# Reordering late products, half-sums and a small norm in a fused linear-attention and GEGLU kernel

## The chip, the cores and the metric

The kernel runs on one core of a Trainium2 chip. The metric is the device time of one launch in microseconds. A core has TensorE (PE in the profile: matrix products into PSUM), VectorE (DVE), ScalarE (ACT, with the gelu and exp functions), GpSimd (POOL, which does not touch PSUM in this kernel) and SyncE (SP, which here only issues DMA transfers). Each engine takes its instructions in the order in which the program writes them for it; between engines they wait for each other.

## The reference

Two stages follow each other. The inputs q, k, v are 8 batches x 8 heads x 576 positions x 64 channels:

```
q_s = softmax(q) over the 64 channels of a head
k_s = softmax(k) over the 576 positions
x   = q_s @ (k_s^T @ v)           # per batch and head, heads side by side: 4608 x 512
out = (gelu(x @ w_gate) * (x @ w_val)) @ w_out      # 512 -> 1536 -> 512
```

All is given and returned in fp32; the kernel multiplies in fp16 and sums in fp32.

## The kernel before, in words

The 4608 rows are done in nine blocks of 512 rows. Blocks 0 to 7 are the first 512 positions (in the kernel's own order) of batches 0 to 7; block 8 collects the 64 remaining positions of all eight batches. The order is 0, 1, ..., 6, 8, 7 (L531). Within a block the hidden layer has 12 columns of 128 (ht[0] to ht[11]), each gelu(g) * v of 512 rows. While a block is in the products with w_gate and w_val, and then in the one with w_out, the attention part of the next batches is interleaved: loads, exp, norms, transposes, the product of keys and values (`unit_kv4`) and x itself (`unit_x4`).

From block 2 on, some hidden columns are made in pairs (k and k+3) by a Strassen-Winograd scheme: seven half-size products instead of eight, at the price of sums beforehand and afterwards. A pair has four steps, written "k.1" to "k.4" (`pair_step`, L630):

- k.1: product 1 into a bank pga, which ScalarE copies to a second bank pgb; product 5 into pgc, of which a snapshot is taken.
- k.2: product 6 into pga, snapshot on ScalarE; product 3 into pgc; VectorE adds (cc, first half).
- k.3: product 7 into pga, VectorE adds (cc, second half, "eq" or "cc" in the profile); product 2 into pgb, from which ScalarE (gelu, glq) and VectorE make the first 256 rows of ht[k] (`final`); then `upper`: ScalarE's gelu on cc, and a 128x512 product by GpSimd (by VectorE for pair 8) that makes rows 256 to 511 of ht[k] and ht[k+3].
- k.4: product 4 into pga, then `final` for the first 256 rows of ht[k+3].

Other columns are made whole ("8g", "8v": `half`, L620): four matmuls each for g and v, gelu on ScalarE, one product on VectorE.

The order of the steps is written out by hand in three strings (L611 to L616): THREE for block 2 (three pairs), FOUR for blocks 3 to 6 (four pairs), SIX for blocks 7 and 8 (six pairs, all columns). `go_on` (L691) walks through a string. Letters in it are places where a list of other work (`plan`, filled by `at`) is run by `ride`; a list may be empty. Four of them matter here: s0, u0, s1, u1 are the half-sums of ht that the product with w_out needs, since that one is a Strassen-Winograd product too (`sum_h`, L566): sj is sum 1 on VectorE and sum 3 on GpSimd, uj is sum 2 on VectorE and sum 4 on GpSimd; j = 1 covers columns 1, 4, 7, 10. The letter t is the DMA transpose of the next batch's normalised q (`unit_td`), and r, in block 6 alone, is the norm of the remaining positions of batch 0 (`norm_rem0`, L268: a VectorE reduce and reciprocal, a GpSimd product) with its DMA transpose (`unit_trem`, L374).

Some work is put off by one step: `live["late"]` holds a function that `go_on` calls after the next item of the string. Two kinds are put off: the `upper` of pair 8 (L680), and the `final` of a k.4 step if the very next item of the string ends in ".1" (L686).

The output stage is `out_strassen` (L728): product 1 into bank a (with the last step or steps k.4 between its matmuls: 2.4 in blocks 3 to 6, 8.4 in blocks 7 and 8), product 2 into b, 5 into c, 6 into a, 3 into c, 7 into a, 4 into a, each of 12 matmuls of 256 columns. `snap` takes a copy of a bank before the next product adds to it; `add` writes rows of the output; the half-sums of columns 2, 5, 8, 11 come between (`last_js`). Product 1 needs ht[0] to ht[5], product 2 needs ht[6] to ht[11], in the order 0, 3, 1, 4, 2, 5. Places NS 0, 1, 2, 4 are where other work rides along: NS 1 is after product 5, NS 2 after product 6. At NS 2 VectorE also makes some of the weight sums (`sum_wgv`) that pairs 7 and 8 of blocks 8 and 7 use.

PSUM has eight banks, handed out in rotation (`big`); a pair's banks are given back by `let_go` when the last reader is written in the program.

Of the kernel before, what the change touches and what calls it, by code (L numbers as in the profile page):

```python
# [18 lines left out]
def kernel(  # L19
# [12 lines left out]
    B, H, S, D = q.shape  # L32
# [16 lines left out]
    NO = NFI // 2  # L49
# [30 lines left out]
    def big(shape, dt, name, hold=False, seed=False):  # L80
        tag = ring.pop(next(i for i, x in enumerate(ring) if x in full) if seed else 0)
        t = ps_big.tile(shape, dt, name=name, tag=tag)
        words = 1
        for n in shape[1:]:
            words *= n
        (full.add if words == 512 and shape[0] == 128 and dt == f32 else full.discard)(tag)
        if hold:
            held[id(t)] = (t, tag)
        else:
            ring.append(tag)  # L90
        return t
# [29 lines left out]
    for i, nm in enumerate("gv"):  # L121
        n = 3 * NO * P
# [472 lines left out]
    def product_gv(i, ps, xt, k, first):  # L595
# [3 lines left out]
        for t, w, nm in ((0, wv_sb, "v"), (1, wg_sb, "g")):  # L599
            ss = ws[(nm, k // NO)]  # L600
            for c in range(2):
# [6 lines left out]

    THREE = ("a 6g l 6v 0.1 9g 0.2 9v w 0.3 7g 0.4 n m 1.1 t 7v 1.2 10g 1.3 s0 10v 1.4 2.1 u0 8g 2.2 s1"  # L611
             " 8v 2.3 u1 11g 2.4 11v x")
    FOUR = ("a 7g l 7v n 0.1 6.1 0.2 6.2 0.3 6.3 m 10g 0.4 6.4 1.1 t 10v 1.2 s0 8g u0 1.3 8v 1.4 r 2.1"
            " 11g s1 2.2 11v 2.3")
    SIX = ("0.1 6.1 0.2 6.2 0.3 6.3 0.4 1.1 6.4 7.1 s0 1.2 7.2 1.3 u0 7.3 1.4 2.1 7.4 8.1 2.2"
           " 8.2 2.3 s1 8.3 u1 2.4")  # L616
    steps = {b: (SIX if b >= B - 1 else THREE if b == 2 else FOUR).split() for b in range(2, B + 1)}
    live = {}

    def half(b, xt, c, nm):  # L620
        t = big([P, 512], f32, "ps" + nm)
        mm_gv(t, wg_sb if nm == "g" else wv_sb, xt, c, range(HP))
        if nm == "g":
            live[c] = ffn.tile([P, 512], f32, name="gl", tag="gl")
            nc.scalar.activation(out=live[c], in_=t, func=ACTF.Gelu)
        else:
            nc.vector.scalar_tensor_tensor(out=ht[:, c, :], in0=t, scalar=_H_SCALE,
                                           in1=live[c], op0=ALU.mult, op1=ALU.mult)
# [62 lines left out]
    def go_on(b, xt, upto=None):  # L691
        while steps[b] and upto != 0:
            x = steps[b].pop(0)
            late = live.pop("late", None)
            if "." in x:
                k, i = x.split(".")
                pair_step(b, xt, int(k), int(i))
                upto = upto - 1 if upto else None
            elif x[-1] in "gv" and x[:-1].isdigit():
                half(b, xt, int(x[:-1]), x[-1])  # L700
            else:
                ride(b, PR, x)
            if late:
                late()
# [3 lines left out]
    def product(i, ps, first, ts=(0, 1), js=range(NO)):  # L708
        for j in js:
            for t in ts:  # L710
                c0, c1 = slice(t * P, (t + 1) * P), slice(256 + t * P, 256 + (t + 1) * P)
                a = {1: ht[:, j, c0], 2: ht[:, NO + j, c0], 3: s4[:, j, c0], 4: ht[:, NO + j, c1],
                     5: sh[1][:, j, c0], 6: sh[2][:, j, c0], 7: ht[:, j, c1]}[i]
                w = {1: wo_sb[:, j, 0:256], 2: wo_sb[:, NO + j, 0:256],
                     3: wo_sb[:, NO + j, 256:512]}.get(i)
                if w is None:
                    w = tw[{4: 4, 5: 1, 6: 2, 7: 3}[i]][:, j]
                nc.tensor.matmul(ps[t], a, w, start=(first and j == js[0] and (  # L718
                    t == ts[0] or ps[t].tensor is not ps[ts[0]].tensor)),
                                 stop=(j == js[-1]), skip_group_check=True)  # L720

    def get_x(b):
        return get_xt(b) if b < B else xtr
# [4 lines left out]
    def out_strassen(b, last):  # L728
        yo = [yop.tile([P, 2, C], f32, name="yo", tag="yo") for _ in range(2)]
        c = (slice(0, 256), slice(256, 512))  # L730
        ps, tiles_ = {}, {}

        def get(nm):
            if last:
                tiles_[nm] = [big([P, 256], f32, "ps" + nm, True) for _ in range(2)]
                ps[nm] = [x for x in tiles_[nm]]
            else:
                tiles_[nm] = [big([P, 2, 256], f32, "ps" + nm, True)]
                ps[nm] = [tiles_[nm][0][:, t] for t in range(2)]

        def parts(nm):
            return [(0, ps[nm][0]), (1, ps[nm][1])] if last else [(slice(0, 2), tiles_[nm][0])]

        def snap(nm, act=False):
            sn = ffn.tile([P, 2, 256], f32, name="sn", tag="gl")
            for n, (t, src) in enumerate(parts(nm)):
                if n or act:
                    nc.scalar.activation(out=sn[:, t], in_=src, func=ACTF.Copy, scale=1.0 / _H_SCALE)
                else:
                    nc.vector.tensor_scalar(out=sn[:, t], in0=src, scalar1=1.0 / _H_SCALE,  # L750
                                            scalar2=None, op0=ALU.mult)
            return sn

        def add(nm, sn, half, col):
            for t, src in parts(nm):
                nc.vector.scalar_tensor_tensor(  # L756
                    out=yo[half][:, t, c[col]], in0=src, scalar=1.0 / _H_SCALE,
                    in1=sn[:, t], op0=ALU.mult, op1=ALU.add)

        js = (0, 1, 2, 3, 4, 5) if b < 2 else (0, 3, 1, 4, 2, 5)  # L760
        get("a")
        four = 2 < b < B - 1
        cut = 3 if four else 4
        product(1, ps["a"], True, js=js[:cut])
        if four:
            pair_step(b, get_x(b), NO // 2 - 1, 4)
            product(1, ps["a"], False, js=js[cut:4])
        ride(b, NS, 0)
        if four:
            ride(b, PR, "u1")  # L770
        if b >= B - 1:
            pair_step(b, get_x(b), NFI - NO // 2 - 1, 4)
        get("b")
        product(1, ps["a"], False, js=js[4:])
        if b > 1 and not last:
            s1 = snap("a", True)
        ride(b, PR, "e")
        sum_h(*last_js(b), (1, 2))
        if b < 2 or last:
            s1 = snap("a")  # L780
        product(2, ps["b"], True, js=js)
        add("b", s1, 0, 0)
        for x in tiles_["b"]:
            let_go(x)
        sum_h(*last_js(b), (4,), "pool" if b > 1 else "dve")
        get("c")
        product(5, ps["c"], True, js=js)
        sum_h(*last_js(b), (3,), "pool" if b > 1 else "dve")
        s5 = snap("c", b == B)
        ride(b, NS, 1)  # L790
        product(6, ps["a"], False, js=js)
        s2 = snap("a", b == B)
        ride(b, NS, 2)
        cut = NO - 1 if 1 < b < B - 2 else NO
        product(3, ps["c"], False, js=js[:cut])
        if cut < NO:
            product(7, ps["a"], False, js=js)
            add("a", s5, 1, 1)
            product(3, ps["c"], False, js=js[cut:])
        add("c", s2, 0, 1)  # L800
        for x in tiles_["c"]:
            let_go(x)
        store_rows(b, 0, yo[0])
        if last:
            finish_last(b, ps["a"], yo[1], s5)
            return
        if cut == NO:
            product(7, ps["a"], False, js=js)
            add("a", s5, 1, 1)
        ride(b, NS, 4)  # L810
        if b == B:
            go_on(B - 1, get_x(B - 1), 1)
        product(4, ps["a"], False, js=js)
        nc.scalar.activation(out=yo[1][:, :, c[0]], in_=tiles_["a"][0], func=ACTF.Copy,
                             scale=1.0 / _H_SCALE)
        let_go(tiles_["a"][0])
        store_rows(b, 1, yo[1])
# [97 lines left out]
    FI, NS, PR = range(3)  # L915
    plan = {}

    def at(b, kind, i, *fns):
        plan.setdefault((b, kind, i), []).extend(fns)

    L = lambda f, *a: (lambda: f(*a))
# [39 lines left out]
    for b in range(2, B):  # L961
        n = b + 1
# [8 lines left out]
            at(b, PR, "e", L(exp, "q", n + 1), L(exp, "k", n + 1))  # L971
    at(4, PR, "l", load_rem0)
    at(4, PR, "e", exp_rem0)
    at(6, PR, "r", norm_rem0, L(unit_trem, 0))
    for b in range(2, B - 1):
        n = b + 1
        at(b, NS, 4, L(unit_x4, n, ("act", "dve"), 0 if n == B - 1 else None))
# [9 lines left out]
    for i, xs_ in (("w", ("g1", "v1", "g2", "v2")), ("x", ("g4", "v4", "g3", "v3"))):  # L987
        for x in xs_:
            at(2, PR, i, L(sum_wgv, x[0], int(x[1]), NO, 1, "pool"))
    for b, x in ((3, "g1"), (3, "g2"), (4, "v1"), (4, "v2"), (5, "g4"), (5, "v4"), (6, "g3"), (6, "v3")):  # L990
        at(b, NS, 2, L(sum_wgv, x[0], int(x[1]), NO + 1, 2))


    def ride(b, kind, i):
        for fn in plan.get((b, kind, i), []):
            fn()

    for b in order:
# [9 lines left out]
        if b > 1:  # L1008
            go_on(b, xt)
# [50 lines left out]
```

## Time and profile before

| | us |
|---|---|
| median of 13 runs | 300.62 |
| lowest, highest | 299.01, 302.50 |
| profiled execution, its own time | 300.53 |
| its span, first to last instruction | 298.7 |
| TensorE busy in the span | 285.1 |
| VectorE busy | 225.9 |
| GpSimd busy | 206.6 |
| ScalarE busy | 194.0 |
| the two weight sums g4, v4 at NS 2 of block 5 (starts) | 198.75, 199.48 |
| norm of batch 0's remainder in block 6 (start of the reduce) | 218.14 |

In the 13 runs the times were 300.53, 299.04, 302.5, 299.17, 299.15, 299.36, 300.77, 300.87, 299.01, 300.7, 302.3, 300.62 and 300.76.

How to read it: the profile's page gives busy times per engine, the clock granted to TensorE in 40 slices, and groups of instructions with the idle time ahead of them and what ended it. Rows in order of time have the start and the length in us, the engine, the source line, the operation, the names it writes and reads, the shapes, and in brackets the idle time before it and what released it. A row may merge several instructions in succession ("x2"). Matmul ends are modelled, so the starts tell more than the lengths. Windows give, for each stretch, its length, the busy time and number of instructions of PE, PEld (weight loads), DVE, ACT and POOL, then the granted clock and the DMA share and rate. Block 2's own steps lie at about 82 to 102 us, its output to 112; blocks 3 to 6 follow every 30 us; block 8 ends its steps at about 252, block 7 at about 284.

### The profile page before, as it was taken

The page shows a single profiled execution, that of the slowest core. Times are in us where ns is not written, and L with a number is a line of the kernel's source. Part 1 is how long each engine was busy: PE and PEld are TensorE (multiplying, and loading weights), DVE is VectorE, ACT ScalarE, POOL GpSimd, SP SyncE. Part 2 cuts the span into 40 slices and gives each one's busy share as a digit, 9 for nine tenths or more (in the row PEclk, how much of TensorE's full clock was granted, in tenths as well). Part 3 has the DMA queues.
Part 4 walks back from the last instruction along what each step waited for, and adds up shares of the span by engine and source line. Part 5 has one row for each costly group of instructions (what it writes and reads, how often), then busy time and mean ns, then how long its engine had stood idle before and what let it go on. Part 6 is the DMA issues. An engine that isn't in the chain of part 4 may idle for free.

```text
span 298.7 us, 6345 instructions
## 1 busy us (share of the span) xinstructions
PE 285.1 (95%) x2449; PEld 204.1 (68%) x2449; DVE 225.9 (76%) x411; ACT 194.0 (65%) x319; POOL 206.6 (69%) x191
## 2 busy tenths in 40 slices
PE   3999999999999999999999999999999998899974
PEld 1544445446766687678767876787678887688864
DVE  2954888978867759768976897689788799449982
ACT  3763467777776398759875987598760777146720
POOL 1558658860599799868986898689875666824570
PEclk9999999999999999999999999999999999799999
DMA  7999999996179307950796069503040300041003
GB/s 223 372 383 390 401 389 395 336 313 195 59 232 346 74 1 248 376 84 0 229 383 112 0 218 383 107 2 143 3 96 2 140 2 1 2 102 41 1 2 140
DMA packets 54622, 51.72 MB, mean 173 GB/s; under 512 B 18496, under 2 KB 50496, under 8 KB 54592
## 3 DMA queue, kind: packets, MB, share of 16 engines
q1 hardware_dynamic: 52864, 49.49, 52.3%
q10 hardware_dynamic: 1728, 1.84, 1.9%
q8 instruction: 19, 0.31, 0.4%
q14 instruction: 11, 0.09, 0.1%
HBM read 37.75 MB, written 9.44 MB: 158 GB/s over the span
## 4 chain that ended last, share of the span: by engine, by line
PE 86%; DVE 7%; ACT 3%; POOL 1%; issue 1%; ACTq 1%; DVEq 0%
PE pga L606 15%; PE psa L718 13%; PE psv L467 12%; PE psg L467 12%; PE pgc L606 8%; PE psc L718 7%; PE psb L718 4%; PE pgb L606 4%; PE psy L535 3%; PE pswarm L459 2%; PE pskv L343 2%; DVE cc L647 1%; DVE sh L576 1%; DVE ht L653 1%; ACT snq L643 1%
## 5 line engine op out<-in xcount | busy, mean ns | idle before, releaser
L467 PE MATMUL psg<-xt,wg_sb 128*128 128x512 f16 x184 | 49.3, 379 | 0.0
L467 PE MATMUL psv<-xt,wv_sb 128*128 128x512 f16 x184 | 49.2, 379 | 0.0
L718 PEld LDWEIGHTS <-ht 128*128 128x128 f16 x384 | 37.0, 99 | 12.6 <-DVE ht L634 4.8
L250 POOL TENSOR_TENSOR eq<-eq,rrq 128x640 f16<-128x640 f16 (+1 forms) x27 | 34.7, 1304 | 11.7 <-DVE rrq L242 7.3
L653 POOL TENSOR_TENSOR ht<-eq 128x512 f16<-128x512 f32 x14 | 17.8, 1273 | 21.3 <-ACT eq L651 21.3
L606 PEld LDWEIGHTS <-wv_sb 128*128 128x128 f16 x248 | 24.1, 98 | 10.1 <-issue 1.9
L467 PEld LDWEIGHTS <-wv_sb 128*128 128x128 f16 x184 | 17.9, 98 | 18.0 <-issue 0.8
L576 POOL TENSOR_TENSOR s<-ht,sh 128x512 f16<-128x512 f16 x21 | 25.6, 1218 | 6.2 <-DVE sh L576 6.2
L576 POOL TENSOR_TENSOR ht<-ht 128x512 f16<-128x512 f16 x21 | 25.6, 1217 | 5.9 <-DVE sh L576 5.9
L467 PEld LDWEIGHTS <-wg_sb 128*128 128x128 f16 x184 | 18.0, 98 | 16.5
L188 POOL CAST v<-vt 128x640 f16<-128x640 f32 x26 | 19.4, 787 | 12.8 <-PE pskv L343 11.3
L606 PEld LDWEIGHTS <-wg_sb 128*128 128x128 f16 x248 | 24.2, 98 | 2.8
L634 DVE SCALAR_TENSOR_TENSOR ht<-pga,glq 128x256 f16<-128x256 f32 x31 | 12.9, 422 | 16.0 <-ACT glq L633 15.9
L472 ACT ACTIVATE gl<-psg 128x512 f32<-128x512 f32 x24 | 13.8, 598 | 16.8 <-PE psg L467 16.8
L653 POOL TENSOR_TENSOR ht<-cc 128x512 f16<-128x512 f32 x15 | 19.1, 1274 | 7.6 <-ACT cc L651 7.5
L633 ACT ACTIVATE glq<-pgb 128x256 f32<-128x256 f32 x31 | 11.7, 378 | 18.7 <-PE pgb L606 10.9
L718 PE MATMUL psa<-tw,ht 128*128 128x256 f16 x192 | 23.4, 273 | 0.3 <-DVE yo L756 0.2
L473 DVE SCALAR_TENSOR_TENSOR ht<-psv,gl 128x512 f16<-128x512 f32 x24 | 16.1, 688 | 9.5 <-PE psv L467 7.6
L212 ACT ACTIVATE ek<-kt 128x1280 f16<-128x1280 f32 (+1 forms) x11 | 19.1, 1748 | 5.4 <-DMA kt<-in_k_dram 3.9
L663 ACT COPY pgb<-pga 128x512 f32<-128x512 f32 x31 | 18.0, 580 | 5.2 <-PE pga L606 5.0
L718 PEld LDWEIGHTS <-sh 128*128 128x128 f16 x192 | 19.3, 100 | 2.7
L643 ACT ACTIVATE snq<-pga 128x512 f32<-128x512 f32 x31 | 18.5, 598 | 4.0 <-PE pga L606 3.7
(172 smaller groups left out, 732.2 us busy)
## 6 DMA issues: line engine op xcount, KB each, us to landing
out_dram<-yo SPq DMA_DIRECT2D x15, 512.0 KB, 3.4
kt<-in_k_dram SPq DMA_DIRECT2D x7, 640.0 KB, 9.3
vt<-in_v_dram SPq DMA_DIRECT2D x7, 640.0 KB, 5.9
qt<-in_q_dram SPq DMA_DIRECT2D x7, 640.0 KB, 7.8
qt<-in_q_dram SPq DMA_DIRECT2D x8, 512.0 KB, 8.2
wost<-in_moe_w_out_dram SPq DMA_DIRECT2D x6, 512.0 KB, 7.9
kt<-in_k_dram SPq DMA_DIRECT2D x6, 512.0 KB, 9.9
vt<-in_v_dram SPq DMA_DIRECT2D x6, 512.0 KB, 6.2
```

Of the source, the lines that this page charges most:

```text
L188: nc.gpsimd.tensor_copy(out=dst, in_=src)
L212: nc.scalar.activation(out=dst[:, n0:NC, h0 * D:h1 * D].rearrange(o, d=D, **({"t": 2} if b >= QUAD else {})), in_=heads(tiles[(nm, b)], b, ...
L250: (nc.gpsimd if eng == "pool" else nc.vector).tensor_tensor(out=e, in0=e, in1=rrq.unsqueeze(-1).to_broadcast((P, n, 2, D)), op=ALU.mult)
L467: nc.tensor.matmul(ps, w[:, ci, fi * P:(fi + 1) * P], xt[:, ci, :], start=(ci == 0), stop=(ci == HP - 1))
L472: nc.scalar.activation(out=gl, in_=psg, func=ACTF.Gelu)
L473: nc.vector.scalar_tensor_tensor(out=ht[:, fi, :], in0=psv, scalar=_H_SCALE, in1=gl, op0=ALU.mult, op1=ALU.mult)
L576: (nc.gpsimd if eng == "pool" else nc.vector).tensor_tensor(out=o, in0=a, in1=b, op=op)
L606: nc.tensor.matmul(ps[:, t], a, x, start=(first and t == 0 and c == 0), stop=(c == 1), skip_group_check=True)
L643: nc.scalar.activation(out=sn, in_=ps, func=ACTF.Copy, scale=_H_SCALE)
L653: (nc.vector if k == NFI - NO // 2 - 1 else nc.gpsimd).tensor_tensor(out=ht[:, k:k + NO // 2 + 1:NO // 2, 256:512], in0=cc[:, :, 0], in1=c ...
L663: nc.scalar.copy(out=pb, in_=pa)
L718: nc.tensor.matmul(ps[t], a, w, start=(first and j == js[0] and (t == ts[0] or ps[t].tensor is not ps[ts[0]].tensor)), stop=(j == js[-1]), ...
```

## The change

- In THREE, s1 moves from between 2.2 and 8v to after 2.3, and u1 from before 11g to after it.
- In FOUR, r is gone, so that 1.4 is directly followed by 2.1.
- In SIX, u1 moves behind 2.4.
- `go_on` keeps a put-off function until the next item that is a pair step, where before any item released it. So in SIX the upper product of pair 8, put off at 8.3, is written after 2.4 and ahead of u1; before, it was written after u1 and ahead of 2.4. In FOUR the final of 1.4 is now put off and written after 2.1.
- In the output stage of block 6, the snapshots of products 5 and 6 are taken by ScalarE; before, by VectorE.
- The norm of batch 0's remainder moves from block 6's steps to NS 1 of block 5's output; its DMA transpose moves to t of block 6, behind that of batch 7.
- The weight sums g4 and v4 move from NS 2 of block 5 to NS 1 of block 6.

```diff
-    THREE = ("a 6g l 6v 0.1 9g 0.2 9v w 0.3 7g 0.4 n m 1.1 t 7v 1.2 10g 1.3 s0 10v 1.4 2.1 u0 8g 2.2 s1"
-             " 8v 2.3 u1 11g 2.4 11v x")
-    FOUR = ("a 7g l 7v n 0.1 6.1 0.2 6.2 0.3 6.3 m 10g 0.4 6.4 1.1 t 10v 1.2 s0 8g u0 1.3 8v 1.4 r 2.1"
+    THREE = ("a 6g l 6v 0.1 9g 0.2 9v w 0.3 7g 0.4 n m 1.1 t 7v 1.2 10g 1.3 s0 10v 1.4 2.1 u0 8g 2.2 8v"
+             " 2.3 s1 11g u1 2.4 11v x")
+    FOUR = ("a 7g l 7v n 0.1 6.1 0.2 6.2 0.3 6.3 m 10g 0.4 6.4 1.1 t 10v 1.2 s0 8g u0 1.3 8v 1.4 2.1"
             " 11g s1 2.2 11v 2.3")
     SIX = ("0.1 6.1 0.2 6.2 0.3 6.3 0.4 1.1 6.4 7.1 s0 1.2 7.2 1.3 u0 7.3 1.4 2.1 7.4 8.1 2.2"
-           " 8.2 2.3 s1 8.3 u1 2.4")
+           " 8.2 2.3 s1 8.3 2.4 u1")
...
-            late = live.pop("late", None)
+            late = live.pop("late", None) if "." in x else None
...
-        s5 = snap("c", b == B)
+        s5 = snap("c", b == B or b == B - 2)
         ride(b, NS, 1)
         product(6, ps["a"], False, js=js)
-        s2 = snap("a", b == B)
+        s2 = snap("a", b == B or b == B - 2)
...
-    at(6, PR, "r", norm_rem0, L(unit_trem, 0))
+    at(5, NS, 1, norm_rem0)
+    at(6, PR, "t", L(unit_trem, 0))
...
-    for b, x in ((3, "g1"), (3, "g2"), (4, "v1"), (4, "v2"), (5, "g4"), (5, "v4"), (6, "g3"), (6, "v3")):
-        at(b, NS, 2, L(sum_wgv, x[0], int(x[1]), NO + 1, 2))
+    for b, i, x in ((3, 2, "g1"), (3, 2, "g2"), (4, 2, "v1"), (4, 2, "v2"), (6, 1, "g4"), (6, 1, "v4"),
+                    (6, 2, "g3"), (6, 2, "v3")):
+        at(b, NS, i, L(sum_wgv, x[0], int(x[1]), NO + 1, 2))
```

## The prediction

> **What bounds the kernel now.** I read the page first, then the waits, then TensorE, VectorE, ScalarE and GpSimd in order of time wherever TensorE pauses. The page:
>
> ```profile
> span 298.7 us, 6345 instructions
> PE 285.1 (95%) x2449; PEld 204.1 (68%) x2449; DVE 225.9 (76%) x411; ACT 194.0 (65%) x319; POOL 206.6 (69%) x191
> PEclk9999999999999999999999999999999999799999
> L718 PEld LDWEIGHTS <-ht 128*128 128x128 f16 x384 | 37.0, 99 | 12.6 <-DVE ht L634 4.8
> ```
>
> TensorE is the bound, so only its pauses can be won. One slice has a lower clock. The last line names the biggest pauses: output products waiting for ht of line 634, 4.8 us in two waits. The waits from 248 to 256 us, and VectorE and TensorE there (end of block 8):
>
> ```profile
> PE psa L718 <- DVE ht L634: 2.1, 1, 2.1
> ```
> ```profile
> 251.99 0.42 DVE L634 SCALAR_TENSOR_TENSOR ht<-pgb,glq 128x256 f16<-128x256 f32 x1
> 252.32 0.84 DVE L576 TENSOR_TENSOR sh<-sh,ht 128x512 f16<-128x512 f16 x1
> 253.09 1.63 DVE L653 TENSOR_TENSOR ht<-cc 128x512 f16<-128x512 f32 x1
> 254.65 0.74 DVE L634 SCALAR_TENSOR_TENSOR ht<-pga,glq 128x256 f16<-128x256 f32 x2
> ```
> ```profile
> 252.61 0.38 PE L718 MATMUL psa<-wo_sb,ht 128*128 128x256 f16 x2
> 255.12 0.39 PE L718 MATMUL psa<-wo_sb,ht 128*128 128x256 f16 x2 [2.13 <-DVE ht L634]
> 255.34 2.35 PE L718 MATMUL psb<-wo_sb,ht 128*128 128x256 f16 x12
> ```
>
> VectorE works through: ht[8], sum 2 of h (u1), the late upper product of pair 8, then ht[5] and ht[11] in one row. Product 1 needs ht[5] and stands from 252.83 to 255.12: 2.3 us. Block 7 repeats it at 284.4 to 286.71. Windows of 3.41 us around the first pause:
>
> ```profile
> 252.37:255.78 3.41, 1.28 (x12) 0.90 (x11) 3.41 (x6) 1.15 (x4) 3.37 (x3) 1.00 0.00 0
> 255.78:259.19 3.41, 3.41 (x18) 2.43 (x16) 1.35 (x3) 0.42 (x1) 2.63 (x3) 0.50 0.02 5
> 259.19:262.61 3.42, 3.42 (x33) 3.06 (x32) 0.09 (x1) 1.19 (x2) 3.34 (x4) 1.00 0.00 0
> ```
>
> The mostly idle window is followed by one at clock 0.50 with 18 matmuls where a full one holds 33: some 1.7 us lost. Block 7's pause brought no such window. The 13 times fall into groups 299.0 to 299.4 (5), 300.5 to 300.9 (6), 302.3 to 302.5 (2), steps of 1.6: none, one or two slow windows. The profiled time, 300.53, is in the middle group, as is the median, 300.62; they may be taken as one. The span leaves 1.8 us around it, which the change does not touch.
>
> Smaller pauses, TensorE released by VectorE in each, are 0.34 us in block 2 (the row here, its columns being start, length, instruction and idle time before it) and 0.40 in block 6:
>
> ```profile
> 100.39 0.38 PE L606 MATMUL pga<-xs,wv_sb 128*128 128x256 f16 x2 [0.18 <-DVE cc L647]
> ```
>
> [...] VectorE's 128x512 sum takes 0.42 alone and 0.84 in the row above, behind a GpSimd product ending at 252.88. [...]
>
> **Parts, with costs.**
>
> *End of blocks 8 and 7: 8.3, 2.4, late upper, u1.* Nothing is added or removed. ScalarE: the gelu of ht[8] runs 251.44 to 251.81; that of ht[5] now follows (0.37) to 252.18, its product being out at 251.46; then the upper gelu 252.18 to 252.81. VectorE: ht[5] starts at 252.32 (where u1 was), ends 252.74; with 0.06 from writer to reader (161.94 to 162.00 in block 4, shown below), TensorE goes on at 252.83 without a pause, 0.22 for two matmuls, then ten of product 2, to 254.14. The upper product starts at 252.86, against GpSimd's sum 3 (begun 252.84, 1.15 alone): freed about 253.95[...]. Sum 2 0.42 to 254.97, ht[11] 0.42 to 255.31 (starts overlap the last ends by 0.08). Product 2 needs ht[11] in its last step: it pauses 254.14 to 255.37, 1.23 us, and ends 255.59. Before, it would have ended at 255.34 + 1.31 = 256.65 at full clock (block 7's twelve matmuls take 1.31). Gain 1.06. What is late next: sum 1 of pair 2/5 must now pass GpSimd's sum 4 (about 255.0 to 256.15), ends 256.5, and product 5 wants it at 255.59 + 8 x 0.109 = 256.46: lose 0.10. In block 7 half the snapshot of product 1 stands behind both sums on VectorE, to 257.18; product 6 wants the bank at 257.0: lose 0.25. GpSimd's sum 4 and sum 3 end near 257.7 and 258.9 as before; products 3 and 7 reach them at 258.9 and 259.6 or later. Net 0.96 + 0.71 = 1.67. Bounds: 0.4 per block if sum 2 or ht[11] is caught by GpSimd again, 1.4 if the upper product gets in first and sum 2 is not caught.
>
> *The slow window.* The pause shrinks from 2.3 to 1.2 us, so the emptiest window is at least 60% busy. Block 7's window with 2.1 of 3.42 idle already brought none. I take none: 1.7 off the profiled run. Bounds 0 and 1.7.
>
> *Final behind 2.1 in blocks 3 to 6 (the empty or moved r stood between).* ScalarE gives its place at 157.24 to the pgb copy, which cannot start before 157.6, and does the gelu of ht[4] (0.38) after the snapshot, 158.61 to 158.99; the next gelu moves 158.92 to 159.0, the snapshot of product 6 159.41 to 159.49. VectorE: ht[4] at 159.03 to 159.45, sum 1 0.09 later (it waited for GpSimd until 159.28), the cc addition 160.03 to 160.12, hence the second cc addition 161.26 to 161.34. This is the chain that 2.4 waits for:
>
> ```profile
> 161.26 0.68 DVE L647 SCALAR_TENSOR_TENSOR cc<-pga,snq 128x512 f32<-128x512 f32 x1
> ...
> 162.00 0.38 PE L606 MATMUL pga<-xs,wv_sb 128*128 128x256 f16 x2
> ```
>
> It ends at 161.94, 0.06 before its reader: no slack. Cost 0.08 in each of four blocks, 0.32; bounds 0 and 0.15 each. Bank release one step later still leaves seven banks for the three that 2.1 takes, in the same order.
>
> *Block 6 without the norm.* Reduce 0.67, reciprocal 0.20, GpSimd product 1.04, which made sum 1 last 1.25 instead of 0.43; 2.4 paused at 222.01 to 222.52, 0.40 more than in block 4. Gain 0.40 (0.3 to 0.45). The transpose of eq0r now follows that of batch 7 on SyncE: 215.32 + 3.02, then 1.17; the next there is the store at 230.63, its reader is at 231. Cost nothing; without the norm done a block earlier it would hold that queue.
>
> *Norm in block 5's output.* VectorE frees at 197.43; 0.70 + 0.22 pushes the snapshot of product 6 from 198.14 to 198.35, ending 199.04, and product 7 wants the bank at 199.03: lose 0.07 (0 to 0.1). GpSimd's 1.04 delays four casts (3.10) and the sums of x from 202.32 to 202.75; the first is wanted at 204.79. Nothing. The sums of g4, v4 (0.81 + 0.93) leave.
>
> *Block 6's output.* Those sums enter after product 5, two snapshots (0.69 each) go to ScalarE, idle 225.27 to 231.52, 0.60 each. Behind GpSimd until 229.07 the sums may take 1.26 each, ending by 230.4; then the addition of product 3 is late by 0.5 but its successor waits for TensorE until 231.22. Nothing; uncovered, 0.2.
>
> *Block 2: s1 after 2.3, u1 after 11g.* The second cc addition moves from 99.67 to 99.17, so 2.4's pause (99.84 to 100.39, 0.34 above its matmul) goes. But GpSimd's sum 3 (1.12) leaves an idle slot at 99.29 and stands behind the upper product, which comes only 0.5 earlier[...]. GpSimd is 0.6 to 0.95 later to the end of block 2; last sum 4 was out at 107.57, wanted at 108.66, now 0.34 earlier. Slack about 0.7: lose 0 to 0.3. Gain 0.2, bounds 0 and 0.34.
>
> Sum: -1.67 -1.70 +0.32 -0.40 +0.07 -0.20 = -3.58; 300.53 - 3.58 = 296.95, told as 297.0. From the lowest group (299.15) less the 1.88 without the window: 297.3.
>
> **Rivals.**
> A: *the wait moves whole from ht[5] to ht[11].* Everything between them is VectorE's 2.5 us, still done before ht[11]. For: the order. Against: product 2 has ten matmuls of cover. [...] 299.15 - 0.8 - 0.2 = 298.2.
> B: *the slow window stays in half of the runs* with a pause of 1.2: 297.0 + 1.7 = 298.7. Against: block 7 above.
> C: *slower: the final behind 2.1 turns the zero slack at 2.4 into a wait.* To pass 300.62 it must cost more than (3.58 + 0.32) / 4 = 0.98 per block, that is sum 1 on VectorE caught by a whole GpSimd instruction (1.2). At 1.4 it gives 297.0 + 4 x 1.32 = 302.3. Against: GpSimd idles from 159.25 until that very sum.
> D: *more:* sum 2 uncaught and the upper product first: 1.4 a block, final free: 295.9.
>
> **Numbers.** Forecast 0.60 (own range 296.3 to 297.8), A 0.15, B 0.08, C 0.04, D 0.13. About 0.5% is what a measurement here tells from no change: 299.1 to 302.1. A and B reach into it. Faster 0.92, same 0.05, slower 0.03. Eight in ten: 295.7 to 298.5.
>
> **What would show it.** Blocks 8 and 7: no pause before the last psa matmuls, one of about 1.2 us before the last two of psb, VectorE in the order ht, ht, upper, sum 2, ht. No clock slice below 9 near the end. 2.4 of block 2 and block 6 without their 0.3 to 0.4; 2.4 of blocks 3 to 5 some 0.08 later. ScalarE with two snapshots in block 6's output. Wrong if psb waits 2 us or more, if a half-clock window remains, or if psc of block 2 pauses over 0.4 for s.

## The result, and the profile after

The changed kernel takes 296.55 us (median of 11 runs, 296.40 to 296.76). Beside it the kernel before had 299.98 us (median of 48 runs, 298.87 to 302.60). The ratio is 0.9879 with a 95% interval of 0.9851 to 0.9907: faster by 1.2%. The forecast was 297.0 with a range of 295.7 to 298.5.

The times of before lie in three groups 1.6 us apart: 24 of the 48 near 299.1, 15 near 300.7, 9 near 302.4. Their median lies in the gap between the first two groups, at a time that no run had. The times after lie in one group. So what is won depends on the group it is measured from: 2.5 us from the lowest, 4.1 us from the profiled execution (300.53 to 296.40; spans 298.7 to 294.6).

The page after, with the clock line in 40 slices:

```profile
span 294.6 us, 6354 instructions
PE 283.3 (96%) x2449; PEld 202.8 (69%) x2449; DVE 226.1 (77%) x409; ACT 194.6 (66%) x321; POOL 205.8 (70%) x191
PEclk9999999999999999999999999999999999999999
```

No slice has a lower clock any more. TensorE has the same 2449 matmuls, in the same order as before, so the two traces can be laid side by side matmul by matmul, and the steps in their distance tell where time went.

The waits at the end of block 8 after (246 to 256 us; who waits for whom, us in total, times, longest):

```profile
PEld L718 <- DVE ht L634: 1.2, 1, 1.2
PE psb L718 <- DVE ht L634: 0.9, 1, 0.9
```

The pause has left product 1 (psa) and stands in product 2 (psb). TensorE there, in order of time:

```profile
252.07 0.60 PE L718 MATMUL psa<-wo_sb,ht 128*128 128x256 f16 x4
252.51 1.26 PE L718 MATMUL psb<-wo_sb,ht 128*128 128x256 f16 x10
254.67 0.39 PE L718 MATMUL psb<-wo_sb,ht 128*128 128x256 f16 x2 [0.91 <-DVE ht L634]
```

Product 1 runs through. Product 2 stops before its last two matmuls, the ones that need ht[11]: 253.60 (ten matmuls of 0.109 from 252.51) to 254.67, 1.07 us, where product 1 stopped for 2.3. VectorE and, after it, GpSimd in the same stretch:

```profile
251.45 0.42 DVE L634 SCALAR_TENSOR_TENSOR ht<-pgb,glq 128x256 f16<-128x256 f32 x1
251.78 0.42 DVE L634 SCALAR_TENSOR_TENSOR ht<-pga,glq 128x256 f16<-128x256 f32 x1
252.30 0.69 DVE L653 TENSOR_TENSOR ht<-cc 128x512 f16<-128x512 f32 x1
252.91 1.38 DVE L576 TENSOR_TENSOR sh<-sh,ht 128x512 f16<-128x512 f16 x1
254.21 0.41 DVE L634 SCALAR_TENSOR_TENSOR ht<-pga,glq 128x256 f16<-128x256 f32 x1
```
```profile
252.31 1.69 POOL L576 TENSOR_TENSOR ht<-ht 128x512 f16<-128x512 f16 x1
```

The same GpSimd sum before:

```profile
252.84 1.33 POOL L576 TENSOR_TENSOR ht<-ht 128x512 f16<-128x512 f16 x1
```

ht[8] and ht[5] follow each other. The upper product takes 0.69 where it took 1.63: it began at 252.30, 0.01 ahead of GpSimd's sum 3, where before it began 0.25 behind that sum (253.09 against 252.84). Sum 3 then takes 1.69 instead of 1.33, to 254.00, and u1's sum 2 takes 1.38 instead of 0.84, to 254.29. ht[11] waits for all that.

That sum 2 was held by sum 3 is read from the ends. It ends 0.28 us after sum 3 does; before, it ended 0.28 us after a GpSimd product that ended at 252.88. The same holds of every half-sum (L576) and weight sum (L587) that took VectorE over 0.6 us after block 2, 15 in the trace of before and 14 in the one after: each began while a GpSimd instruction ran and ended 0.27 or 0.28 us after it. No kernel here takes sum 3 off GpSimd at this place.

The distances of the two traces step like this (after minus before, us; read from the starts of the same matmul in both):

| place | step |
|---|---|
| start-up, up to 14 us | +0.08 |
| block 2, step 2.4 | -0.29 |
| block 2, product 3 and 7 | +0.07 |
| blocks 3 to 5 | 0 |
| block 6, step 2.4 | -0.39 |
| block 8, product 1 (ht[5]) | -2.29 |
| block 8, product 2 (ht[11]) | +1.07 |
| block 8, slow window and product 5 (rest of the sum) | -1.56 |
| block 7, product 1 (ht[5]) | -2.32 |
| block 7, product 2 (ht[11]) | +1.07 |
| block 7, product 5 and product 6 | +0.08, +0.35 |
| sum | -4.13 |

### The profile page after: what moved, and what is told of

The parts are those of the page before. It is cut to its first block, busy times and chain, and to the rows that moved or that the text cites. A ratio compares the mean times of both kernels' runs of the same rounds, so it can differ in the third digit from the quotient of the medians.

```text
span 294.6 us, 6354 instructions
## 1 busy us (share of the span) xinstructions
PE 283.3 (96%) x2449; PEld 202.8 (69%) x2449; DVE 226.1 (77%) x409; ACT 194.6 (66%) x321; POOL 205.8 (70%) x191
## 5 line engine op out<-in xcount | busy, mean ns | idle before, releaser
L718 PEld LDWEIGHTS <-ht 128*128 128x128 f16 x384 | 36.4, 98 | 10.1 <-issue 2.7
L576 POOL TENSOR_TENSOR ht<-ht 128x512 f16<-128x512 f16 x21 | 26.7, 1269 | 6.1 <-DVE sh L576 6.1
L576 POOL TENSOR_TENSOR s<-ht,sh 128x512 f16<-128x512 f16 x21 | 24.7, 1176 | 6.9 <-DVE sh L576 6.9
L240 DVE TENSOR_REDUCE rq<-eq 128x20 f32<-128x1280 f16 (+1 forms) x12 | 17.2, 1433 | 4.5 <-ACT eq L212 4.5
```

The source lines that it names most:

```text
L240: nc.vector.reduce_sum(rq, e, axis=mybir.AxisListType.X)
L576: (nc.gpsimd if eng == "pool" else nc.vector).tensor_tensor(out=o, in0=a, in1=b, op=op)
```

## The experiments

Each kernel was timed beside the kernel before, in four runs where nothing else is said. All times are medians.

### The end of blocks 8 and 7 alone, and all the rest alone

The first kernel is the one before with these two lines alone:

```diff
-           " 8.2 2.3 s1 8.3 u1 2.4")
+           " 8.2 2.3 s1 8.3 2.4 u1")
...
-            late = live.pop("late", None)
+            late = live.pop("late", None) if "." in x else None
```

> The kernel before with only the end of blocks 8 and 7 changed (late upper product behind 2.4, u1 behind both). Theory (the pause moves from ht[5] to ht[11] and shrinks from 2.3 to 1.1 us, and with it the slow TensorE window never comes): 1.2 us less in block 8, 0.8 in block 7, all times in one group at 297.0 to 297.2, no slice under clock 0.9 near the end. Rival (the slow window has another cause than the long pause): groups 1.6 us apart remain, median 298 to 299. Rival (blocks 2 to 6 hold most of the gain): 299 or more.

The second is the changed kernel with these two lines put back.

> The changed kernel with the end of blocks 8 and 7 put back as before. Theory: only block 2 (0.2 to 0.3) and block 6 (0.4) are won, the two pauses of 2.3 us stay, and about a third of them bring a slow window of 1.6 us: times in groups at about 298.4, 300.0 and 301.7. Rival (slow window has another cause): one group at 298.4 or lower.

The end alone gave 297.06 us (296.93 to 297.23, one group; ratio to before 0.9871, 0.9820 to 0.9922). The rest alone gave 300.13 (298.38 to 302.08; ratio 0.9984, 0.9957 to 1.0011), in groups near 298.5, 300.2 and 301.9 with 6, 9 and 5 of its 20 runs. The lowest of these lies 0.5 to 0.6 under the lowest group of before, which is what blocks 2 and 6 won. So the end of blocks 8 and 7 carries the change, and the groups go with the pause of 2.3 us. The profiled run of the rest alone caught both pauses with a slow window behind each. Windows of that kernel (length, then busy us and number of instructions of PE, PEld, DVE, ACT, POOL, then clock, DMA share and rate), the first with the pause of block 8, then the slow ones behind the pauses of blocks 8 and 7:

```profile
252.83:256.24 3.41, 1.27 (x13) 1.15 (x13) 3.38 (x6) 0.96 (x3) 2.76 (x2) 1.00 0.00 0
256.24:259.65 3.41, 3.41 (x18) 2.44 (x17) 0.78 (x2) 0.09 (x1) 3.24 (x3) 0.50 0.02 5
286.96:290.37 3.41, 3.41 (x19) 2.43 (x17) 2.03 (x5) 0.38 (x1) 2.50 (x3) 0.50 0.02 5
```

The two slow windows begin 30.72 us apart, nine times 3.413. In the kernel before, the clock record shows 0.50 for 3.413 us, full clock for 245.76 us ahead of that and for 40.96 behind it, which is 72 and 12 such windows. So the windows are read below as a regular grid, which can be counted back from a slow one.

### The upper product behind 2.4, u1 where it was

```diff
-           " 8.2 2.3 s1 8.3 2.4 u1")
+           " 8.2 2.3 s1 8.3 u1 2.4")
```

against the changed kernel, whose rule for put-off work stays.

> The changed kernel, but with u1 ahead of 2.4 again, the late upper product still behind 2.4. Theory (ht[11] sets the end whatever the order ahead of it, since the same VectorE work lies ahead of it): ht[5] comes 0.7 us later and pauses product 1 by that, product 2 then pauses only 0.2 us for ht[11]; time 296.4 to 296.8, the same as the changed kernel. Rival (each instruction that goes ahead of ht[5] costs its length): 0.7 us in each block, 298.0.

It gave 296.08 us (296.00 to 296.26). The pauses have the theory's shape, but the time is 0.5 less than that of the changed kernel and below the theory's range. VectorE at the end of block 7 of this kernel:

```profile
280.15 0.41 DVE L634 SCALAR_TENSOR_TENSOR ht<-pgb,glq 128x256 f16<-128x256 f32 x1
280.48 0.85 DVE L576 TENSOR_TENSOR sh<-sh,ht 128x512 f16<-128x512 f16 x1
281.25 0.41 DVE L634 SCALAR_TENSOR_TENSOR ht<-pga,glq 128x256 f16<-128x256 f32 x1
281.59 1.30 DVE L653 TENSOR_TENSOR ht<-cc 128x512 f16<-128x512 f32 x1
282.82 0.41 DVE L634 SCALAR_TENSOR_TENSOR ht<-pga,glq 128x256 f16<-128x256 f32 x1
```

Product 1 pauses 0.75 us for ht[5] again, but product 2 then begins later and loses 0.8 less at ht[11]; the matmuls beyond run 0.1 to 0.25 earlier than in the changed kernel, and product 6 of block 7 another 0.14. From the start of ht[8] to that of ht[11] VectorE needs 2.67 us here (280.15 to 282.82) and 2.75 in block 7 of the changed kernel (280.24 to 282.99). What pays is thus the upper product behind 2.4; moving u1 as well gained nothing and cost about 0.2 us in each block.

### ht[11] ahead of all sums

```diff
-           " 8.2 2.3 s1 8.3 2.4 u1")
+           " 8.2 2.3 s1 8.3 2.4")
...
-        sum_h(*last_js(b), (1, 2))
+        sum_h(*last_js(b), (1,))
+        if b >= B - 1:
+            ride(b, PR, "u1")
+        sum_h(*last_js(b), (2,))
```

> The changed kernel with u1 taken behind ht[11] and behind the last sum 1 as well (VectorE: ht[5], upper, ht[11], sum 1 of columns 2 and 5, u1, sum 2). Theory (the new pause of 1.1 us is sum 2 of u1 held by GpSimd's sum 3, 1.38 us, ahead of ht[11]): no pause in product 2; product 6 of block 7 pauses 0.3 for its snapshot and product 7 of block 7 up to 0.4 for GpSimd's sum 3; 1.7 us less than the changed kernel, 294.8 to 295.3. Rival (the sums themselves set the end, the pause only moves to product 5, 6 or 3): 296.2 to 296.6.

It gave 294.15 us (294.06 to 294.41; ratio to before 0.9777, 0.9716 to 0.9838), 2.4 less than the changed kernel. TensorE at the end of block 7 of this kernel, and VectorE:

```profile
280.18 1.47 PE L718 MATMUL psb<-wo_sb,ht 128*128 128x256 f16 x12
281.49 1.47 PE L718 MATMUL psc<-tw,sh 128*128 128x256 f16 x12
283.01 1.47 PE L718 MATMUL psa<-tw,sh 128*128 128x256 f16 x12
```
```profile
279.97 0.69 DVE L653 TENSOR_TENSOR ht<-cc 128x512 f16<-128x512 f32 x1
280.57 0.42 DVE L634 SCALAR_TENSOR_TENSOR ht<-pga,glq 128x256 f16<-128x256 f32 x1
280.91 1.04 DVE L576 TENSOR_TENSOR sh<-ht 128x512 f16<-128x512 f16 x1
281.87 0.75 DVE L576 TENSOR_TENSOR sh<-sh,ht 128x512 f16<-128x512 f16 x2
```

Product 2 runs through. Side by side with the changed kernel, 1.03 and 1.08 us go at its last two matmuls in blocks 8 and 7, 0.08 in product 5 of each, and 0.14 in product 6 of block 7. So the 1.07 us left by the change came from sum 2 of u1, held by GpSimd, standing ahead of ht[11]. Here ht[11], which reads one input from PSUM, takes its 0.42 us while GpSimd's sum 3 still runs (279.98 to 281.66); the held one is now sum 1 behind it, with 1.04 us to 281.95. My expectation of 1.7 us less was 0.7 too small: I had charged product 7 with up to 0.4 for GpSimd's sum 3, and it took 0.07; products 5 and 6 gave 0.30 that I had not counted.

### The snapshot of block 7 on ScalarE, and its last sum 3 on VectorE

```diff
-            s1 = snap("a")
+            s1 = snap("a", last)
```

on top of the kernel with ht[11] first.

> The kernel of the run with ht[11] first, and the snapshot of product 1 in block 7 taken by ScalarE alone. Theory (the 0.2 us by which product 6 of block 7 still starts late is that snapshot's half behind three sums on VectorE): 0.2 us less than with ht[11] first, 293.8 to 294.1. Rival (product 6 is late for another reason, sum 2 or the bank): 294.1 to 294.4, no change.

294.17 us (294.02 to 294.39): the rival's number, by another way. In the trace product 6 of block 7 starts 0.18 us earlier, and product 7 is 0.21 later against it, so nothing remains. The next kernel takes that last wait away as well:

```diff
-        sum_h(*last_js(b), (3,), "pool" if b > 1 else "dve")
+        if not last:
+            sum_h(*last_js(b), (3,), "pool" if b > 1 else "dve")
...
         s2 = snap("a", b == B or b == B - 2)
+        if last:
+            sum_h(*last_js(b), (3,))
```

> As the run with ht[11] first and ScalarE's snapshot, and in block 7 the last sum 3 on VectorE behind the snapshot of product 6. Theory (what the snapshot gave, 0.2 us, was taken back because product 7 waits for GpSimd's last sum 3, behind two sums 4): product 7 starts its third column at once, 0.2 us less, 293.8 to 294.1. Rival (product 7 waits for the bank or for something else): 294.0 to 294.4, no change.

293.95 us (293.79 to 294.19; ratio to before 0.9758, 0.9687 to 0.9830). In the trace the step is there: 0.29 us go within product 7. In the times 0.2 us is no more than their spread, and the profiled runs differ by 0.3 in start-up alone; a gain of this one edit is not shown by the times.

### A longer pause

```diff
         if b >= B - 1:
+            nc.vector.reduce_sum(att.tile([P, 2], f32, name="pad", tag="rck"), wo_sb[:, 0:2, :],
+                                 axis=mybir.AxisListType.X)
             pair_step(b, get_x(b), NFI - NO // 2 - 1, 4)
```

> The changed kernel with one needless VectorE reduce of 1024 elements (about 1.2 us, its result unused) ahead of ht[11] in blocks 8 and 7. Theory (a pause of 2.3 us of TensorE brings a slow window in about a third of the cases, one of 1.1 us never, whatever TensorE waits for): both pauses in product 2 grow to 2.2 to 2.4 us, the lowest times are 298.8 to 299.1, and groups 1.6 us higher appear again. Rival (the slow window belonged to the wait in product 1 or to VectorE's load of before): one group at 298.8 to 299.1.

The median of seven runs is 298.52 us, in two groups: 298.15 to 298.52 (4 runs) and 299.74 to 299.94 (3 runs). The lowest is 0.6 below what I had expected, since the wait of 0.35 us in product 6 of block 7 vanishes behind the longer pause, and the reduce cost 1.1 rather than 1.2 of pause in each block. The profiled run has one slow window. Windows before and behind the two pauses (253.7 to 255.92 and 283.55 to 285.75), first those of block 8, then those of block 7:

```profile
251.67:255.08 3.41, 2.21 (x21) 1.67 (x18) 3.31 (x5) 1.61 (x3) 3.05 (x3) 1.00 0.02 5
255.08:258.49 3.41, 2.57 (x24) 2.32 (x25) 2.14 (x5) 0.60 (x1) 2.31 (x3) 1.00 0.00 0
282.39:285.80 3.41, 1.37 (x14) 0.99 (x12) 3.41 (x5) 0.66 (x2) 2.71 (x2) 1.00 0.00 0
285.80:289.21 3.41, 3.41 (x17) 2.43 (x18) 2.17 (x6) 0.26 (x1) 2.26 (x2) 0.50 0.02 5
```

The windows of block 8 are counted back from the slow one, nine windows earlier. The pause of block 8 falls across their border, TensorE is busy for at least 2.21 of 3.41 us in each, and the clock stays. That of block 7 falls into one window and the next runs at half clock. So a pause of this length brings the slow window back, in product 2 as in product 1, and in these traces it depends on how the pause lies to the grid of windows. Executions of one kernel differ in whether it comes.

### The final at once in blocks 3 to 6, and the norm back in block 6

The first has an empty place r between 1.4 and 2.1 of FOUR, so that the final of 1.4 is written at once as before; the second has the norm and its transpose there again.

```diff
-    FOUR = ("... 1.3 8v 1.4 2.1"
+    FOUR = ("... 1.3 8v 1.4 r 2.1"
```

> The changed kernel with an empty place r between 1.4 and 2.1 in blocks 3 to 6, so that the final of 1.4 is written at once as before. Theory from the trace after (ScalarE's snapshot of product 6 kept its place, the short gelu hides in ScalarE's gaps): no difference, 296.4 to 296.8. Rival (the prediction's step: 0.08 us per block is lost by the late final): 0.3 us less, 296.2 to 296.3.

```diff
-    at(5, NS, 1, norm_rem0)
-    at(6, PR, "t", L(unit_trem, 0))
+    at(6, PR, "r", norm_rem0, L(unit_trem, 0))
```

> As the run with the final at once, and the norm of batch 0's remainder with its transpose put back at r in block 6. Theory (GpSimd's 1.04 us product holds VectorE's sum 1, which pushes the cc addition that 2.4 waits for): 0.4 us more than the run with the final at once, 296.8 to 297.1. Rival (the gain in block 6 came from the sums or the snapshots moved there): no difference.

The final at once gives 296.52 us (296.22 to 296.59), no difference from 296.55. With the norm back too it is 296.93 (296.70 to 297.07), 0.4 more, and the two traces part by 0.35 us at step 2.4 of block 6 and nowhere else behind start-up. VectorE there with the norm back:

```profile
218.27 0.67 DVE L271 TENSOR_REDUCE rq<-eq0r 64x8 f32<-64x512 f16 x1
219.56 1.24 DVE L576 TENSOR_TENSOR sh<-ht 128x512 f16<-128x512 f16 x1 [0.39 <-POOL ht L653]
```

Sum 1 takes 1.24 us behind GpSimd's norm product (1.25 before), and 0.35 of that reaches TensorE.

### The snapshots of block 6 back on VectorE

```diff
-        s5 = snap("c", b == B or b == B - 2)
+        s5 = snap("c", b == B)
...
-        s2 = snap("a", b == B or b == B - 2)
+        s2 = snap("a", b == B)
```

> The changed kernel with the two snapshots of block 6's output back on VectorE, the sums g4 and v4 still at NS 1 of block 6. Theory (ScalarE's snapshots are what makes room for these sums: in the trace after, VectorE is busy with them from 226.7 to 229.6 without a gap, and GpSimd holds two of them): the snapshot of product 6 ends at 229.3 to 229.7 where product 7 wants its bank at 229.17, a pause of 0.2 to 0.6 us, time 296.7 to 297.1. Rival (the snapshots' place costs nothing either way): 296.4 to 296.7, no new pause in product 7.

297.40 us (297.40 to 297.52), 0.85 more than the changed kernel. VectorE in block 6's output, with v4 ahead of the snapshot, and TensorE:

```profile
227.78 1.37 DVE L587 TENSOR_TENSOR kt<-wv_sb,kt 128x512 f16<-128x512 f16 x1
229.08 0.68 DVE L750 TENSOR_SCALAR sn<-psa 128x512 f32<-128x512 f32 x1
```
```profile
229.81 1.47 PE L718 MATMUL psa<-tw,ht 128*128 128x256 f16 x12 [0.39 <-DVE sn L750]
```

The snapshot ends at 229.76 and product 7 waits for it: 0.55 us, within the expected pause of 0.2 to 0.6. With the moved sums at this place, the snapshots on ScalarE thus save that much. The time is 0.3 above the expected range, because of one step more. That second step, of 0.35 us, lies in pair 2 of block 8, where VectorE's addition of 8.2 starts later than in the changed kernel; nothing in this edit touches it, and its cause stays open.

## Why the prediction was right, step by step

The forecast of 297.0 was 0.45 us above the measured median, and the sum against the profiled execution was -3.58 where -4.13 was measured. By the terms:

- **Blocks 8 and 7, product 1 to product 2.** Forecast: the pause moves from ht[5] to ht[11] and shrinks to 1.23 us, net gain 0.96 and 0.71. Measured: 1.07 us, net gain about 1.14 and 0.82 (2.29 - 1.07 - 0.08, taking for block 8 the 0.08 of product 5 that the comparison with ht[11] first shows there; 2.32 - 1.07 - 0.43). The mechanism is shown by the two halves of the change, by ht[11] first, and by u1 put back. I had the wrong one of VectorE and GpSimd first, on a forecast difference of 0.02 us (252.84 against 252.86), which was too small to decide it: the upper product went ahead of sum 3 and took 0.69, and sum 2 paid with 1.38. My 1.06 had sum 3 first. It and the pause of 1.23 also rest on a length of the upper product behind sum 3 that the trace of before does not show: there that product took 1.63, begun beside sum 3. The forecast pause for that order and the measured one for this differ by only 0.16 us. That both orders put the same work ahead of ht[11] would explain it, but no kernel here has the forecast order at that place, so this is argued and not shown. The part of the 2.3 us that stayed is rival A's mechanism, at half its size.
- **The slow window.** Forecast: none left, 1.7. Measured: none in any run of the changed kernel, about 1.6 (1.56 and the 0.08 it hid). Rival B is refuted for pauses of 1.07 us, and the kernel with a longer pause shows that the pause, not the place, is what matters. The longest stretch of pause inside one window without a slow one behind it was 2.08 us (block 7 before, 284.42 to 286.50), the shortest with one 2.14 (the rest alone, 252.83 to 254.97), counted from 0.109 us after the last matmul's start: the border lies near there, by these two cases.
- **The final behind 2.1, +0.32.** This step was wrong in size: 0 in blocks 3 to 5, and 0 by the run with the final at once. The term that failed is ScalarE's: I let the 0.38 us gelu of ht[4] hold the next gelu for its whole length, 158.61 to 158.99, but the next starts 0.28 behind it. ScalarE of block 4 after:

```profile
158.49 0.39 ACT L633 ACTIVATE glq<-pga 128x256 f32<-128x256 f32 x1
158.77 0.61 ACT L625 ACTIVATE gl<-psg 128x512 f32<-128x512 f32 x1
159.26 0.60 ACT L643 ACTIVATE snq<-pga 128x512 f32<-128x512 f32 x1
```

  With block 4 running 0.15 earlier than before, the snapshot at 159.26 is where it was (159.41), so the addition behind it is not late either. Sum 1 does come 0.13 later, but VectorE was idle after it until that snapshot. The rival of a slower kernel had the same root and fell with it.
- **Block 6 without the norm, -0.40.** Measured -0.39, and +0.35 when it was put back.
- **The norm in block 5's output, +0.07.** Measured 0: the snapshot behind it starts 0.12 after the reciprocal, not 0.22, and ends in time.
- **Block 6's output, 0.** Measured 0. GpSimd held v4 for 1.37 and the sums ended at 229.67; the addition of product 3 was not late, because ScalarE had the snapshots. Without them product 7 paused 0.55 us.
- **Block 2, -0.20.** Measured -0.29 and +0.07, the second where GpSimd's late sums 4 and 3 are wanted, as forecast.

The 0.55 us between the two sums are thus the final (0.32), blocks 8 and 7 (0.29), the norm in block 5 (0.07) and block 2 (0.02), less the slow window (0.06), a later start-up that was not forecast (0.08) and block 6 (0.01). The mechanism was right; the largest single error was a cost that did not arise.

## What to carry to other kernels

When a stall is one of order, list what the engine does between the two results that the bound engine waits for: moving one piece behind the first result shifts the wait to the second, and as long as that one comes no sooner, it pays only for the matmuls that lie between (twelve of 0.109 us here, 1.31 in all, of which 1.22 were won). Put ahead of the last awaited result only what it needs; here one sum held by GpSimd cost 1.07 us per block there and almost nothing behind it. A long pause of TensorE could cost twice here, 2.3 us itself and, in some executions, 1.6 us in the clock afterwards, so several groups of times in one kernel are a reason to look for a pause with a slow window behind it.

## What the runs showed of the hardware

- In these traces TensorE ran at clock 0.50 for one window of 3.41 us behind a long pause: behind that of block 8 before (2.29 us, from 252.83 to 255.12), those of blocks 8 and 7 in the rest alone (2.14 us of the first lie in the window ahead of the slow one) and that of block 7 with the longer pause (2.20, from 283.55 to 285.75). The windows ahead had 1.28, 1.27 and 1.37 of 3.41 us busy in the first, second and fourth case. Block 7 before, with 2.08 us of pause and 1.50 busy in its window, had no slow window behind it. In the slow window of before the matmuls of product 2 started 0.213 us apart, against 0.109 at full clock.
- A VectorE sum of two SBUF operands took 0.42 us alone, 1.38 beside GpSimd's sum 3 (252.91 after) and 1.55 beside a GpSimd product (100.78 in block 2 after). The upper product took 0.69 where it began 0.01 or 0.02 us ahead of sum 3 (blocks 8 and 7 after, block 7 with ht[11] first), 1.63 where it began 0.25 behind it (both blocks before) and 1.30 where it began 0.58 behind (block 7 with u1 put back).
- On ScalarE the instruction behind one of 0.39 us started 0.28 after it (158.49 and 158.77 in block 4 after).
- VectorE took its instructions in the order in which they are written: at the end of block 8 ht[8], sum 2, upper product, ht[5] before (251.99, 252.32, 253.09, 254.65), and ht[8], ht[5], upper product, sum 2, ht[11] after (251.45, 251.78, 252.30, 252.91, 254.21).
